# An S4 convolution block with a gated bilinear unit: low powers from exponentials, seeds earlier, the first block's gate on the result, one set of row statistics, and modulation rows behind the first products

## The chip, the cores and the metric

The kernel runs on one core of one Trainium2 chip, in 32-bit floats. The metric is the device time of one execution in microseconds, given as a median over runs. A core has a matrix engine (PE; its weight loads are listed as PEld), a vector engine (DVE), an activation engine (ACT), a general engine (POOL) and a synchronising engine (SP) that here issues nearly all transfers (DMA). Each engine runs its own instructions strictly in order and waits where an operand or a buffer isn't ready yet.

## The reference, cut to what matters

```python
mod = (silu(c) @ w_mod).reshape(1, 6, 1, 640)
sa, ca, ga, sb, cb, gb = (mod[:, i] for i in range(6))
h = layernorm(x) * (1 + ca) + sa                 # x: 2048 x 640
# S4: one kernel of 2048 taps per channel, from 192 complex modes
dt = exp(log_dt); A = A_re + 1j * A_im
K[d, l] = Re(sum_n C[d, n] * exp(dt[d] * A[d, n] * l) * dt[d] * B[d, n])
y = causal_convolution(h, K) + h * Dskip         # over the 2048 rows, by FFT of 4096
x = x + ga * y
h = layernorm(x) * (1 + cb) + sb
x = x + gb * (((h @ w_gate) * (h @ w_up)) @ w_down)   # 640 -> 1536 -> 640
```

## The kernel before, in words

The 640 channels are five blocks (db) of 128. The kernel K is made in 40 steps of 16 channels (n = 0 to 39; a half block hf is four such steps). The power of a mode at tap l is magnitude times phase, and both are split into a low part (l modulo 8) and high parts, so that a step needs only small tables and outer products:

- *Seeds* (`u_seeds`, L597 to L769) prepare a block: rho = dt * A_re and the phase step, the product B*C, its magnitude amp (a root) and its angle (an arctangent), all transposed on PE so that modes lie along partitions. The steps are named by letters and run in the order of the strings SEG0 (block 0, before the main loop) and SEG (later blocks, spread over the loop): `l` loads, `a` rho and phase, `b` and `c` the product B*C and transposes, `u` and `x` the magnitude, `d`/`D` the phase tables DL and DH of half 0 and 1, `r`/`R` the multiples RL and RH of rho, `e`/`E` the exponentials, `f`, `G`, `g`, `h`, `v` amplitude, arctangent and starting phase.
- *Low tables*: LP (seven exponentials of 64*l*rho, on ACT), LH (`tab_ph`, integer phases, POOL) and LQ (`tab_eq`, POOL: amp, amp times the first power, and two doublings). LQ has one copy, so it can only be made after the last use of the one before.
- *Outer products* on POOL (`outer`, L817): Ph (phases, 3.1 us), EQ (3.1 us) and EP (1.65 us) per step n. ACT turns phases into cosine and sine (`trig`, three calls per step: `kg_aq`, `kg_ap`, `kg_b`), DVE multiplies them with EQ and EP (QtA, PtA, PtB, QtB; L872, L878, L898), and PE adds the products up in the bank kg (`kg_ma` L913, `kg_mb` L928). Two PSUM buffers tra and trb take turns for the trig results; Ph, EQ and EP have two copies each.

Meanwhile the layer norm runs over 16 row blocks q: `u_stats` loads block q and takes its statistics on DVE (L568), `row_stats` turns them into reciprocal roots (a root on ACT, between two table loads), `u_hm` normalises on ACT and writes hm to memory. The row blocks from 6 on, loaded once for the statistics and again for the normalising, share three buffers gha, ghb, ghc, in the order a, b, c, a, a, c, a, b, c for blocks 13, 15, 7, 6, 10, 11, 14, (7 again), 12. A load into a buffer waits for the statistics of the block that it replaces.

The modulation vectors come from `mod_l(m)`, which loads 640 columns of w_mod (1.6 MB) into the tables t_tw (m = 2, 0, 4) or t_ti (m = 1, 3, 5), `u_modr`, which multiplies them on PE in two parts (384 and 256 columns, ten products each, L458) and copies the rows out on ACT, and `u_fold`, which turns the rows of m = 0, 1, 2 into columns by 1x1 products (L477), works out shift, gate and their quotients on DVE (L481 to L491) and spreads them again. Rows 3 and 4 follow in `u_modc`.

The transforms (`u_pre` L955, `u_k`, `u_g`, `u_c`, `u_d`) are PE products with activation copies and trips through memory between them; from about 500 us on the gated unit runs on PE almost alone (L1196, L1611).

What runs when is written out by hand in SCHED: each unit is a generator, and each number is the time of one of its steps. The number divided by 1000 is the slot. Slots from -101 on belong to the steps of block 0's seeds, slots 2t and 2t+1 to iteration t of the main loop (three iterations per n), before and after the loop's DVE products:

```python
    for t in range(3 * NK + 24):
        n, g = divmod(t, 3)
        ...
            (kg_aq, kg_ap, kg_b)[g](n)
        due(2 * t)
        ...
            for f in MUL.pop(0):
                f()
        due(2 * t + 1)
        if g < 2 and n + 1 < NK:
            kg_pool(n + 1, g)
```

SLOT lists the buffer that each allocation takes. The order of emission is the order on every queue, SP's included.

## Time and profile before

| | us |
|---|---|
| median of three runs | 992.87 |
| lowest, highest | 990.01, 998.23 |
| the profiled execution's own time | 990.33 |
| its span in the trace | 988.6 |

| engine | busy us | share of the span |
|---|---|---|
| PE | 887.3 | 90% |
| PEld | 726.3 | 73% |
| DVE | 760.7 | 77% |
| ACT | 579.9 | 59% |
| POOL | 577.4 | 58% |

The span leaves out 1.7 us of that execution's time. Times in the lines below are us from the span's start. A line of the timeline has the start, the busy time, the engine, the line of the kernel, the operation, output<-input by the program's names, the tile, and the count where several are merged; in brackets stands how long the engine had been idle and what ended that. A name such as gha is the buffer a of the ring gh. SPq is the issue of a transfer on SP; what a transfer takes is told by those who wait for it.

### The profile page before, as it was taken

Reading aid. Unit: us, or ns where it says so; the run is one execution under the profiler, and the core shown is the slowest. Engines: PE = TensorE matmul, PEld = TensorE weight load, DVE = VectorE, ACT = ScalarE, POOL = GpSimd, SP = SyncE. Lnnn points to the kernel's source line nnn. Section 1 sums busy time; section 2 is a strip of 40 time slices with the busy share of each in tenths; the row PEclk is TensorE's granted clock in tenths of the full one; section 3 lists DMA queues with packets and bytes.
Section 4 is the critical chain, followed back from the end, with each engine's and each line's share of the span. In section 5 each row is a group of like instructions: output and inputs, shape, how many; then the busy total and the mean of one; then the engine's idle time right before and its main releaser. Section 6 shows DMA issues by size and latency. Waiting matters only on the chain.

```text
span 988.6 us, 26668 instructions
## 1 busy us (share of the span) xinstructions
PE 887.3 (90%) x11190; PEld 726.3 (73%) x11190; DVE 760.7 (77%) x1311; ACT 579.9 (59%) x1019; POOL 577.4 (58%) x424
## 2 busy tenths in 40 slices
PE   4854898999798699989988999999999999999998
PEld 3643656676575477677666888889998888889998
DVE  8798479887988977896899877787585977677452
...
GB/s 243 240 172 196 224 211 205 142 138 120 142 151 142 172 155 106 183 187 281 217 102 106 134 186 104 137 159 168 198 134 216 85 80 80 81 54 77 83 161 54
DMA packets 141961, 148.96 MB, mean 151 GB/s; under 512 B 8976, under 2 KB 120080, under 8 KB 140432
## 3 DMA queue, kind: packets, MB, share of 16 engines
...
## 4 chain that ended last, share of the span: by engine, by line
PE 58%; DVE 14%; ACT 13%; issue 6%; POOL 5%; DMA 2%; SPq 0%; DVEq 0%; ACTq 0%; POOLq 0%
PE pa L1196 26%; PE pa L1611 16%; ACT tra L320 2%; ACT trb L320 2%; PE psfb L995 2%; DVE QtA L872 2%; PE psfc L995 2%; PE psfb L1055 1%; PE kg L928 1%; POOL EQ L817 1%; PE psfa L1055 1%; PE kg L913 1%; PE psfc L1055 1%; PE psfb L950 1%; PE psfa L995 1%
## 5 line engine op out<-in xcount | busy, mean ns | idle before, releaser
L817 POOL TENSOR_TENSOR EQ<-LQ,RH 128x1536 f32<-128x1536 f32 x40 | 124.2, 3105 | 15.1 <-DVE QtB L872 14.9
L320 ACT ACTIVATE z<-pa 128x512 f32<-128x512 f32 x24 | 14.4, 599 | 167.1 <-PE pa L1196 120.5
L1160 DVE TENSOR_TENSOR wsgl<-wga,wsgh 128x640 fp32r<-128x640 f32 x72 | 68.1, 948 | 46.8 <-ACT wsgh L320 46.6
L320 ACT ACTIVATE wsgh<-wga 128x640 fp32r<-128x640 f32 x72 | 52.6, 732 | 72.0 <-PE pa L1611 48.6
L1560 POOL TENSOR_TENSOR z<-z,s 128x512 f32<-128x512 f32 x24 | 33.5, 1394 | 98.6 <-DVE s L1559 98.6
L1611 PE MATMUL pa<-wsgh,sh 128*128 128x384 f32 (+1 forms) x304 | 69.6, 310 | 0.0
L1611 PE MATMUL pa<-wsgh,sl 128*128 128x384 f32 (+1 forms) x304 | 69.2, 308 | 0.0
L1611 PE MATMUL pa<-wsgl,sh 128*128 128x384 f32 (+1 forms) x304 | 69.1, 309 | 0.0
L1172 POOL TENSOR_TENSOR tf<-wur,wgb 128x256 f32<-128x256 f32 x24 | 19.2, 801 | 80.7 <-DVE wtl L1160 54.7
L817 POOL TENSOR_TENSOR EP<-LP,RH 128x768 f32<-128x768 f32 x40 | 66.1, 1652 | 0.0
L817 POOL TENSOR_TENSOR Phb<-LH,DH 128x1536 int32<-128x1536 int32 x20 | 62.3, 3113 | 2.2 <-ACT tra L320 2.1
L817 POOL TENSOR_TENSOR Pha<-LH,DH 128x1536 int32<-128x1536 int32 (+1 forms) x21 | 62.4, 2972 | 1.8 <-ACT trb L320 1.4
L872 DVE TENSOR_TENSOR QtA<-tra,EQ 128x1024 f32<-128x1024 f32 x40 | 47.0, 1216 | 17.0 <-ACT tra L320 8.5
L1160 DVE TENSOR_TENSOR wtl<-tf,wth 128x256 fp32r<-128x256 f32 (+1 forms) x72 | 59.9, 858 | 0.0
L872 DVE TENSOR_TENSOR QtA<-trb,EQ 128x1024 f32<-128x1024 f32 x40 | 47.0, 1215 | 12.2 <-ACT trb L320 7.0
L928 PE MATMUL kg<-QtB,PtB 64*32 64x64 f32 x2560 | 47.0, 225 | 8.1 <-DVE QtB L872 8.0
L928 PEld LDWEIGHTS kg<-QtB,PtB 64*32 64x32 f32 x2560 | 40.3, 112 | 15.5 <-DVE QtB L872 9.0
L1558 DVE TENSOR_TENSOR s<-pa,s 128x512 f32<-128x512 f32 x24 | 16.6, 690 | 45.2 <-PE pa L1196 40.1
L1196 PE MATMUL pa<-sl,wth 128*128 128x512 f32 x144 | 45.2, 395 | 2.1 <-DVE sl L1160 2.1
L1611 PEld LDWEIGHTS pa<-wsgh,sl 128*128 128x128 f32 x304 | 46.6, 188 | 0.0
L1611 PEld LDWEIGHTS pa<-wsgh,sh 128*128 128x128 f32 x304 | 46.5, 188 | 0.0
L1611 PEld LDWEIGHTS pa<-wsgl,sh 128*128 128x128 f32 x304 | 46.5, 188 | 0.0
...
## 6 DMA issues: line engine op xcount, KB each, us to landing
...
```

The source lines that it names most:

```text
L320: return S.activation(o, i, f, **kw)
L817: G.tensor_tensor(o.rearrange("p x (h l) -> p x h l", l=8), lo.unsqueeze(2).to_broadcast([P, rows, nh, 8]), hi.rearrange("p h x -> p x h") ...
L872: return [lambda h=h: V.tensor_tensor(Qt[:, :, :, 32 * h : 32 * h + 32], tr[:, ::-1] if h else tr[:, :, :, ::-1], e[:, :, 32 * h : 32 * h ...
L928: PE.matmul(kg[j * 32 : j * 32 + 32, dd, :], PtB[lo : lo + 64, c, r, :], QtB[lo : lo + 64, c, r, :], start=False, stop=dd == 7 and c == 1, ...
L995: PE.matmul(r[c][par * 64 : par * 64 + 64, i, :], t_tw[:, k0 + k, c, :], src[:, k, :], start=True, stop=True, tile_position=(0, par * 64))
L1055: PE.matmul(r[par][:, i], w, v, start=c == 0, stop=c == 1, tile_position=(lo, 0))
L1160: V.tensor_tensor(lo, v, hi, op=OP.subtract)
L1172: G.tensor_tensor(t[:, 0:2], u[:, 0:2], g[:, 0:2], op=OP.subtract)
L1196: PE.matmul(ps, w[a][:, k], x[b][:, l], start=n == 0 and m == 0, stop=n == 2 and m == len(ks) - 1)
L1558: V.tensor_tensor(S67[i], ps, S6[i], op=OP.add)
L1560: G.tensor_tensor(ZT[i], ZT[i], S67[i], op=OP.add)
L1611: PE.matmul(ACC[tb][t][c], x[:, ts], w[:, cs], start=st, stop=f == NF - 1 and n == 2 and (c == 0 or t % 2 == 1))
```

## The change

It has eight parts.

1. LQ is no longer made on POOL. `s_e` gets seven more exponentials (l*rho for l = 1 to 7) in place of one over three multiples of rho, and a new step `q` multiplies them by amp on DVE. `tab_eq` goes; LQ has three copies; RL holds rho alone.
2. The order of block 0's seeds (SEG0): the amplitude and arctangent run earlier, the half 1 tables (`D`) later, and half 1's exponentials (`X`) move from the main loop to the seeds. POOL's outer products EP(1) and EQ(0) and the phases of half 0 are issued inside the seeds, in another order.
3. The statistics of blocks 1, 13, 6, 7, 10 and 15 get later slots, behind the seeds.
4. Modulation products: half of row 1 and all of row 0 move from the seeds to slots 6, 7 and 8 of the main loop, and the loads of w_mod for rows 3 and 4 to slots 6 and 8. The fold moves from slots 11, 12, 19, 22 to 12, 14, 18, 20.
5. One `row_stats` for 16 row blocks in place of two (6 and 10).
6. The gate of block 0 multiplies the result in `u_d` (DVE, in PSUM) and no longer the input in `u_pre` (POOL).
7. `trig` puts the magnitude of the phase into the PSUM buffer that later holds the cosine, where before it had a buffer ab of its own.
8. Smaller: the starting phase of a later block takes three POOL operations for four; temporaries of the seeds share space; three phase tables share a row of zeros.

```diff
@@ -30,24 +30,24 @@
 
 SCHED = dict(
     ml=(-88998, -91999, -98999),
-    mr=(((-87997, 8001), (-87996, 11000)), ((-87999, 2000), (-88997, 8000)), ((-88999, -86998), (-89000, -87998))),
+    mr=(((7000, 11000), (8000, 12000)), ((-87999, 2000), (6000, 9000)), ((-88999, 1100), (-89000, 100))),
     st=(
         (-88993, 5000),
-        (-101000, -92000),
+        (-101000, -87500),
         (5001, 22003),
         (-88996, 15002),
         (-98997, 0),
         (10000, 21002),
-        (-94000, -87995),
-        (-98000, -87994),
+        (-94000, -85900),
+        (-98000, -85800),
         (1000, 20000),
         (1, 19000),
-        (-91998, -87000),
+        (-91998, -85700),
         (-88995, 6000),
         (-87993, 13000),
-        (-99000, -91000),
+        (-99000, -87400),
         (-88994, 16001),
-        (-98998, -86999),
+        (-98998, -85600),
     ),
...
@@ -67,12 +67,11 @@
         (44001, 53002),
         (35002, 43001),
     ),
-    rstd=(22004, 22005),
+    rstd=(22004,),
     tab=(52000, 78002),
-    fo=(11001, 12000, 19001, 22000),
-    e0=(15000,),
+    fo=(12800, 14500, 18001, 20001),
     ds=(32001, 21000, 34000, 43002),
-    mc=((-86997, 21003, 30001, 33001, 37002), (-87992, 39001, 45000, 46001, 48001), (34004, 56000, 60001)),
+    mc=((6500, 21003, 30001, 33001, 37002), (8500, 39001, 45000, 46001, 48001), (34004, 56000, 60001)),
...
-SEG0 = ("l", "a", "b", "c", "ud", "r", "x", "e", "f", "G", "g", "D", "h", "v", "R", "")
-SEG = ("l", "a", "b", "c", "ud", "D", "r", "R", "x", "E", "f", "g", "h", "v")
+SEG0 = ("l", "a", "b", "c", "iud", "r", "x", "e", "f", "Gg", "q", "R", "hv", "DX", "", "Q", "")
+SEG = ("l", "a", "b", "c", "iud", "D", "r", "R", "x", "E", "f", "g", "h", "v")
...
@@ -486,7 +483,6 @@
         V.tensor_tensor(gg, p3[:, 2], g1, op=OP.mult)
-        V.tensor_tensor(sh[:, 0:1], sh[:, 0:1], gg[:, 0:1], op=OP.mult)
         V.tensor_tensor(dt2[:, 1:], dt2[:, 1:], gg[:, 1:], op=OP.mult)
         V.tensor_tensor(dcol[:, 1:], dcol[:, 1:], gg[:, 1:], op=OP.mult)
...
@@ -583,16 +579,17 @@
 
     EQ = [pk1.tile([P, 24, 64], F32, name=f"EQ{i}") for i in range(2)]
     EP = [pk1.tile([P, 24, 32], F32, name=f"EP{i}") for i in range(2)]
-    LQ = pk1.tile([P, 96, 8], F32, name="LQ")
+    LQ = pk1.tile([P, 3, 96, 8], F32, name="LQ")
     LP = pk1.tile([P, 3, 96, 8], F32, name="LP")
     LH = pk1.tile([P, 192, 8], I32, name="LH")
     V.memset(LP[:, :, :, 0], 1.0)
     RH = pk1.tile([P, 3, 11, 96], F32, name="RH")
-    RL = pk1.tile([P, 2, 4, 96], F32, name="RL")
-    DH = [pk1.tile([P, 4, 192], I32, name=f"DH{i}") for i in range(3)]
+    RL = pk1.tile([P, 2, 96], F32, name="RL")
...
@@ -668,29 +664,29 @@
             act(u, x, AF.Square)
             act(q[:, 0], y, AF.Square)
 
+        def s_i():
+            T["st"] = T["q"][:, 1].bitcast(I32).rearrange("p (s r) -> p s r", r=24)
+            V.tensor_copy(T["st"], T["ps"][:, 1])
+
         def s_d(h):
-            ps, q = T["ps"], T["q"]
-            sti = q[:, 1].bitcast(I32).rearrange("p (s r) -> p s r", r=24)
+            ps, sti = T["ps"], T["st"]
             free(h, "lh", "ph")
-            if h == 0:
-                V.tensor_copy(sti, ps[:, 1])
+            if h:
+                V.tensor_tensor(t64, sti, shl[:, 5:6].unsqueeze(2).to_broadcast([P, 8, 24]), op=OP.logical_shift_left)
             V.tensor_copy(g5(Dl[h])[:, 0, :, 1, :], ps[:, 1, hs[h]])
             for a, k0 in ((1, 0), (0, 6)):
                 for D_, n, o in ((Dl[h], 3, 1), (Dh[h], 2, 1)):
                     V.tensor_tensor(g5(D_)[:, o : o + n, :, a, :], sti[:, hs[h]].unsqueeze(1).to_broadcast([P, n, 4, 24]),
                                     shl[:, k0 : k0 + n].unsqueeze(2).unsqueeze(3).to_broadcast([P, n, 4, 24]), op=OP.logical_shift_left)
                     k0 += 3
-            if h:
-                V.tensor_tensor(t64, sti, shl[:, 5:6].unsqueeze(2).to_broadcast([P, 8, 24]), op=OP.logical_shift_left)
             mark("step", 2 * db + h)
 
         def s_r(h):
-            ps = T["ps"]
-            free(h, "ep", "eq", "lq")
-            V.tensor_tensor(g4(Rl[h])[:, 0:3], ps[:, 0, hs[h]].unsqueeze(1).to_broadcast([P, 3, 4, 24]),
-                            mults[:, 11:14].unsqueeze(2).unsqueeze(3).to_broadcast([P, 3, 4, 24]), op=OP.mult)
-            V.tensor_tensor(g4(Rh[h]), ps[:, 0, hs[h]].unsqueeze(1).to_broadcast([P, 11, 4, 24]),
-                            mults[:, 0:11].unsqueeze(2).unsqueeze(3).to_broadcast([P, 11, 4, 24]), op=OP.mult)
+            rho_ = T["ps"][:, 0, hs[h]]
+            free(h, "ep", "eq")
+            V.tensor_copy(Rl[h].rearrange("p (s r) -> p s r", r=24), rho_)
+            V.tensor_tensor(g4(Rh[h]), rho_.unsqueeze(1).to_broadcast([P, 11, 4, 24]),
+                            mults.unsqueeze(2).unsqueeze(3).to_broadcast([P, 11, 4, 24]), op=OP.mult)
 
         def s_u():
             V.tensor_tensor(u, u, T["q"][:, 0], op=OP.add)
...
@@ -702,35 +698,38 @@
             V.tensor_scalar(pe[:, 1], x, 0.0, 0.5, op0=OP.is_ge, op1=OP.subtract)
 
         def s_e(*hh):
-            lp, rh, rl = (halves(R, hh) for R in (LP, RH, RL))
+            lp, lq, rh, rl = (halves(R, hh) for R in (LP, LQ, RH, RL))
             for l in range(1, 8):
-                act(lp[:, :, :, l], rl[:, :, 0], AF.Exp, scale=64.0 * l)
+                act(lp[:, :, :, l], rl, AF.Exp, scale=64.0 * l)
             act(rh, rh, AF.Exp)
-            act(rl[:, :, 0:3], rl[:, :, 0:3], AF.Exp)
+            for l in range(1, 8):
+                act(lq[:, :, :, l], rl, AF.Exp, scale=float(l))
             for h in hh:
                 mark("lp", 2 * db + h)
+
+        def s_q(*hh):
+            lq, a = halves(LQ, hh), T["amp"][:, hh[0] : hh[-1] + 1]
+            V.tensor_copy(lq[:, :, :, 0], a)
+            V.tensor_tensor(lq[:, :, :, 1:8], lq[:, :, :, 1:8], a.unsqueeze(3).to_broadcast([P, len(hh), 96, 7]), op=OP.mult)
+            for h in hh:
+                mark("lq", 2 * db + h)
 
         def s_f():
             pe = T["pe"]
             if db:
                 need(1, "gg")
-            V.scalar_tensor_tensor(amp, u, dt2[:, db : db + 1], pe[:, 1], op0=OP.mult, op1=OP.mult)
             V.scalar_tensor_tensor(pe[:, 0], pe[:, 0], 1e-37, u, op0=OP.max, op1=OP.add)
+            V.scalar_tensor_tensor(u, u, dt2[:, db : db + 1], pe[:, 1], op0=OP.mult, op1=OP.mult)
             V.reciprocal(pe[:, 0], pe[:, 0])
             V.scalar_tensor_tensor(y, y, 2.0, pe[:, 1], op0=OP.mult, op1=OP.mult)
             V.tensor_tensor(pe[:, 0], y, pe[:, 0], op=OP.mult)
             V.tensor_scalar(y, pe[:, 0], 1.0, -1.0, op0=OP.min, op1=OP.max)
 
         def s_G():
-            if db:
-                ps = bank("ps2")
-            else:
-                ps = ring(ps_tr, [P, 2, 512], "tr")[:, :, :N]
+            ps = bank("ps2") if db else ring(ps_tr, [P, 2, 512], "tr")[:, :, :N]
             T["ps2"] = ps.rearrange("p c (s r) -> p c s r", r=24)
-            trans(amp, T["ps2"][:, 0])
-            if db == 0:
-                for h in range(2):
-                    act(g4(Rl[h])[:, 3], T["ps2"][:, 0, hs[h]])
+            T["amp"] = ps[:, 0].rearrange("p (h x) -> p h x", h=2)
+            trans(u, T["ps2"][:, 0])
 
         def s_g():
             if db:
...
@@ -741,26 +740,26 @@
             trans(y, T["ps2"][:, 1])
 
         def s_v():
-            ps = T["ps2"]
             if db:
+                s_q(0, 1)
+            V.tensor_scalar(psi, T["ps2"][:, 1], 4294967296.0 / math.pi, 536870912.0, op0=OP.mult, op1=OP.add)
+
+            def plus(w):
+                G.tensor_tensor(t64[:, w], t64[:, w], psi[:, w], op=OP.add)
+
+            def minus(h):
+                G.tensor_tensor(g5(Dl[h])[:, 0, :, 0, :], t64[:, hs[h]], g5(Dl[h])[:, 0, :, 1, :], op=OP.subtract)
+
+            if db:
+                PSI[2 * db] += [one(plus, slice(0, 8)), one(minus, 0), one(minus, 1)]
+            else:
                 for h in range(2):
-                    V.tensor_copy(g4(Rl[h])[:, 3], ps[:, 0, hs[h]])
-            V.tensor_scalar(psi, ps[:, 1], 4294967296.0 / math.pi, 536870912.0, op0=OP.mult, op1=OP.add)
-
-            def weighted(h):
-                st, s0 = g5(Dl[h])[:, 0, :, 1, :], g5(Dl[h])[:, 0, :, 0, :]
-                G.tensor_tensor(t64[:, hs[h]], t64[:, hs[h]], st, op=OP.subtract)
-                G.tensor_tensor(s0, t64[:, hs[h]], psi[:, hs[h]], op=OP.add)
-
-            for h in range(2):
-                PSI[2 * db + h if db == 0 else 2 * db].append(lambda h=h: weighted(h))
+                    PSI[h] += [one(plus, hs[h]), one(minus, h)]
             mark("seeds", db)
 
         one = lambda f, *a: lambda: f(*a)
-        steps = dict(l=s_l, a=s_a, b=s_b, c=s_c, d=one(s_d, 0), D=one(s_d, 1), r=one(s_r, 0), R=one(s_r, 1), u=s_u, x=s_x,
-                     e=one(s_e, 0), E=one(s_e, 0, 1), f=s_f, G=s_G, g=s_g, h=s_h, v=s_v)
-        if db == 0:
-            LATE.append(lambda: s_e(1))
+        steps = dict(l=s_l, a=s_a, b=s_b, c=s_c, i=s_i, d=one(s_d, 0), D=one(s_d, 1), r=one(s_r, 0), R=one(s_r, 1), u=s_u, x=s_x,
+                     e=one(s_e, 0), X=one(s_e, 1), E=one(s_e, 0, 1), f=s_f, G=s_G, g=s_g, h=s_h, q=one(s_q, 0), Q=one(s_q, 1), v=s_v)
         for i, seg in enumerate(SEG0 if db == 0 else SEG):
             if i:
                 yield
...
@@ -802,16 +801,6 @@
         G.tensor_tensor(lh[..., 1:2], lh[..., 0:1], one(d[1]), op=OP.add)
         double(lh, d[2:], OP.add)
 
-    def tab_eq(hf):
-        need(1, "seeds", hf // 2)
-        if hf:
-            need(1, "eq", 4 * hf - 1)
-        mark("lq", hf)
-        rl = RL[:, hf % 2]
-        G.tensor_copy(LQ[:, :, 0:1], rl[:, 3].unsqueeze(2))
-        G.tensor_tensor(LQ[:, :, 1:2], rl[:, 3].unsqueeze(2), rl[:, 0].unsqueeze(2), op=OP.mult)
-        double(LQ, (rl[:, 1], rl[:, 2]), OP.mult)
-
     def outer(o, lo, hi, rows, nh, op):
 
         G.tensor_tensor(o.rearrange("p x (h l) -> p x h l", l=8),
...
@@ -851,20 +840,21 @@
             mk_ph(n)
             return
         mk_eq(n)
-        mk_ep(n)
+        if n > 1:
+            mk_ep(n)
 
     def trig(src, ab=None):
 
         tr = ring(ps_tr, [P, 2, 512], "tr")
         sv = tr[:, 1, :]
+        cv = tr[:, 0, :]
         if ab is None:
-            ab = pk.tile([P, 512], F32, name="ab", bufs=1)
-            av = ab
+            ab = av = cv
             if len(src.shape) == 3:
                 av, sv = (t.rearrange("p (a x) -> p a x", a=2) for t in (av, sv))
             act(av, src, AF.Abs, scale=TURN)
         act(sv, src, AF.Sin, scale=TURN)
-        act(tr[:, 0, :], ab, AF.Sin, scale=-1.0, bias=halfpi)
+        act(cv, ab, AF.Sin, scale=-1.0, bias=halfpi)
         return tr
 
     def qmul(Qt, tr, e, R):
...
@@ -962,8 +952,6 @@
         SY.dma_start(h, hm[:, 4 * q : 4 * q + 4, db * P : db * P + P])
         yield
         need(1, "sh")
-        if db == 0:
-            G.tensor_tensor(h, h, xa[:, 4, 0:P].unsqueeze(1).to_broadcast([P, 4, P]), op=OP.mult)
         r = [ring(PF[-1], [P, 4, P], "psf") for _ in range(2)]
         d0 = slice(db * P, db * P + P)
         for i in range(2):
...
@@ -1107,6 +1095,8 @@
         mark("d", c)
         if not own:
             need(1, "xr", c, NB - 2)
+        if db == 0:
+            V.tensor_tensor(ps, ps, ggr.unsqueeze(1).to_broadcast([P, 4, P]), op=OP.mult)
         V.tensor_tensor(xs, ps, xs, op=OP.add)
         SY.dma_start(x2d[:, 4 * c : 4 * c + 4, d0], xs)
 
...
@@ -1353,11 +1343,11 @@
         mark("ti")
         SY.dma_start(t_ti.rearrange("p h l m -> p (h l m)"), I["t_ti"])
 
-    def row_stats(q0, q1):
-        need(q1 - q0, "st", q0 == 0)
-        s_ = slice(q0, q1)
-        rstd(mv1[:, s_, :], rs1[:, s_], nm1[:, s_], rv[:, s_], ry[:, s_])
-        mark("rs", q0 == 0)
+    def row_stats():
+        need(10, "st", False)
+        need(6, "st", True)
+        rstd(mv1, rs1, nm1, rv, ry)
+        mark("rs")
 
     def due(x):
         for _, g in sorted(jobs.pop(x, []), key=lambda j: j[0]):
...
@@ -1419,12 +1406,14 @@
             mk_ph(0, 1)
         elif i == P_EP:
             mk_ep(0)
+            mk_ep(1)
+        elif i == P_EQ:
+            mk_eq(0)
+        elif i == P_PSI:
+            tab_ph(0, 0)
+            mk_ph(0, 0)
         elif i == P_MOD:
             mod_i()
-    tab_eq(0)
-    tab_ph(0, 0)
-    mk_ph(0, 0)
-    mk_eq(0)
     for t in range(3 * NK + 24):
         n, g = divmod(t, 3)
         k = n < NK

```

50 lines of the change are left out of this document (23 added, 27 removed).

## The prediction, made before the changed kernel was run

> **What bounds the kernel now.** I read the page's chain first, then the chain for stretches of the span, the busy time by stretch, and the timelines of each queue for the first 100 us, since nearly every edit lies there.
>
> ```profile
> PE 58%; DVE 14%; ACT 13%; issue 6%; POOL 5%; DMA 2%; SPq 0%; DVEq 0%; ACTq 0%; POOLq 0%
> 73.50:150.00 76.50, 57.84 (x1168) 39.77 (x1168) 55.10 (x86) 74.82 (x120) 67.53 (x42) 0.83 0.62 206
> 480.00:988.00 508.00, 493.63 (x2622) 427.46 (x2620) 363.93 (x609) 191.60 (x368) 190.11 (x177) 0.99 0.38 122
> ```
>
> The first line is the chain by engine. The others give, for a stretch, busy us of PE, PE's weight loads, DVE, ACT and POOL, then granted clock, DMA share and GB/s. From 480 on PE is busy 493.6 of 508 us and the change touches nothing there. From 73.5 to 150 ACT is busy 74.8 of 76.5 us: whatever delays ACT's entry into that stretch, or adds to it, delays all that follows. The first 60 us belong to POOL:
>
> ```profile
> by line: POOL EQ L817 16.1%; POOL Phb L817 10.2%; issue 9.8%; POOL Pha L817 7.9%; POOL EP L817 6.9%; POOL LH L777 6.6%; DMA ldt<-A_log_dt 4.2%; DVE st L568 2.8%; DVE DL L680 2.5%; POOL LQ L777 2.4%; DVE psfb L719 2.3%; DVE RH L692 1.9%; POO
> ```
>
> So the change's start (POOL relieved) aims at a real bound there. But other queues run close behind, and the answer lies in them.
>
> **POOL's part.** Rows of POOL, start and duration:
>
> ```profile
> 15.73 1.65 POOL L817 TENSOR_TENSOR EP<-LP,RH 128x768 f32<-128x768 f32 x1
> 17.31 0.36 POOL L811 COPY LQ<-RL 128x96 f32<-128x96 f32 x1
> 18.01 1.51 POOL L777 TENSOR_TENSOR LQ<-LQ,RL 128x192 f32<-128x192 f32 x2
> 26.21 3.09 POOL L817 TENSOR_TENSOR EQ<-LQ,RH 128x1536 f32<-128x1536 f32 x1
> 36.99 3.11 POOL L817 TENSOR_TENSOR Pha<-LH,DH 128x1536 int32<-128x1536 int32 x1
> ```
>
> The low-power table LQ costs POOL 17.31 to 19.52, 2.2 us; ten of them make 22 us. EP(1), 1.6 us, moves into the gap before EQ(0). By queue order EQ(0) then ends near 22.0 instead of 29.3, and phases Pha(0) near 27 (26.3 before), so Ph(1) ends about 2.5 us sooner. That lead is kept only if DVE consumes it.
>
> **DVE's first products come later.** The second half's steps on DVE (L677 to L684, 19.11 to 20.8 below, 1.7 us) now follow q, R and the wait for the transposed arctangent (ACT first does seven more powers, so the arctangent ends near 17.9 instead of 17.4). They end near 21.3, and only then come the row statistics of blocks 1 and 13, which stood ahead of them:
>
> ```profile
> 18.07 0.89 DVE L568 BATCH_NORM_STATS2 st<-gha 128x6 f32<-128x320 f32 x2
> 19.11 0.20 DVE L677 CAST DL<-psfc 128x96 int32<-128x96 f32 x1
> 20.49 0.34 DVE L684 TENSOR_TENSOR ptb<-psfa,shl 128x192 int32<-128x192 int32 x1
> ...
> 18.98 0.33 SPq L560 DMA_DIRECT2D gha<-A_u  x1
> 19.36 0.43 SPq L451 DMA_DIRECT2D t_ti<-w_mod  x1
> ...
> 21.92 0.89 DVE L568 BATCH_NORM_STATS2 st<-gha 128x6 f32<-128x320 f32 x2 [0.82 <-DMA gha<-A_u]
> 22.83 0.33 SPq L560 DMA_DIRECT2D gha<-A_u  x1
> 27.19 0.89 DVE L568 BATCH_NORM_STATS2 st<-gha 128x6 f32<-128x320 f32 x2 [1.50 <-DMA gha<-A_u]
> 30.57 2.31 DVE L872 TENSOR_TENSOR QtA<-trb,EQ 128x1024 f32<-128x1024 f32 x2
> ```
>
> This is a loop through one buffer: statistics free gha, SP loads the next block into it, DVE waits for that. Block 13's statistics end near 23.0 instead of 18.96: 4.0 later. Load 6 goes out then, lands 2.9 later, load 10 after its statistics, landing 4.4 later, and statistics 10, 15 and 4 (3.4 us together) still stand ahead of QtA(0). QtA(0) goes from 30.6 to about 34.6, though its inputs are ready at 26. The t_ti rows queue on SP behind load 6 and come 4.0 later too. The transposed-phase banks and Pha are held until QtA(0) has run, so Pha(2) starts about 1 us late instead of 3.5 early: POOL's lead is gone.
>
> **The fold.** The modulation fold's operations stand on DVE behind PE:
>
> ```profile
> 28.68 3.39 PE L458 MATMUL psfc<-t_ti,sil 128*128 128x384 f32 x10
> 43.39 0.60 PE L477 MATMUL psfb<-ident,TVa 1*128 1x1 f32 x4 [2.45 <-ACT TVa L320]
> 47.22 0.17 DVE L481 TENSOR_SCALAR mcol<-psfb 128x5 f32<-128x5 f32 x1 [2.26 <-PE psfb L477]
> 53.03 1.18 DVE L878 TENSOR_TENSOR PtAa<-tra,EP 128x1024 f32<-128x1024 f32 x1
> ```
>
> Three of six modulation products (3.4 us for 384 columns, by that 2.3 for each of 256) move behind kg(0); with kg's own blocks of 1.1 us PE ends them near 48.7, the last row copy on ACT is near 50.4, the 1x1 products take some 4.2 (in before 43.39 to 47.2, the first few sooner), the DVE operations 2.5 (47.22 to 49.7), so these run 54.6 to 57.2, now ahead of PtA(2). PtA(2) ends near 58 instead of 54.2. Statistics 14, which frees gha for load 8, end 3.75 later.
>
> **SP's queue, the dearest step.** Loads of w_mod for rows 4 and 3 moved from the start to steps 8500 and 6500. They are now behind load 8 and ahead of load 5 (Wb):
>
> ```profile
> 38.64 0.38 SPq L451 DMA_DIRECT2D t_tw<-w_mod  x1
> 51.41 1.40 SPq L451 DMA_DIRECT2D t_ti<-w_mod  x1
> 57.74 0.33 SPq L560 DMA_DIRECT2D gha<-A_u  x1
> 58.59 0.42 SPq L560 DMA_DIRECT2D Wb<-A_u  x1
> 66.33 0.88 DVE L568 BATCH_NORM_STATS2 st<-Wb 128x6 f32<-128x320 f32 x2
> GB/s 259 193 7 0 3 124 331 355 294 321 369 355 376 386 420 399 406 181 65 7 130 389 352 416 365 423 399 420 201 106 273 399 413 413 420 403 413 389 396 399
> ```
>
> The last row is the DMA rate in 40 slices of 5 to 35 us: it tops out near 410. Before, Wb's statistics at 66.33 waited for nothing. Now loads 8 and 2, both tables and load 5 leave together at about 61.9 (57.74 and 3.75, and the issue): blocks of 0.33 MB and tables of 640 x 640 floats, 4.26 MB in all, at 410 is 10.4 us, plus 1.9 for issue and landing (estimate from load 6: 2.9 with 0.8 of transfer): load 5 lands near 74.5 to 75, Wb's statistics are 8.5 later. DVE's seed products, statistics 2 and the root wait behind it in order, and ACT waits for the root:
>
> ```profile
> 70.82 0.21 ACT L320 ACTIVATE ry<-rv 128x6 f32<-128x6 f32 x1
> 72.37 0.21 ACT L320 ACTIVATE ry<-rv 128x10 f32<-128x10 f32 x1 [1.34 <-DVE rv L371]
> 74.83 0.60 ACT L320 ACTIVATE trb<-Pha 128x512 f32<-128x512 int32 x1
> ```
>
> One set of row statistics saves 72.37 less 70.82, 1.5 us, here. ACT enters its saturated stretch 8.5 - 1.5 = 7.0 us late.
>
> **Powers on ACT.** For each later block:
>
> ```profile
> 94.33 2.63 ACT L320 ACTIVATE LP<-RL 128x192 f32<-128x192 f32 x7
> 98.62 0.67 ACT L320 ACTIVATE RL<-RL 128x576 f32<-128x576 f32 x1
> 345.30 2.68 ACT L320 ACTIVATE LP<-RL 128x192 f32<-128x192 f32 x7 [0.20 <-DVE RL L690]
> ```
>
> Seven more of 0.375 (2.63) replace one of 0.67: +2.0 us. At 94 it lies in the saturated stretch, at 345 the chain also runs through LP: +2.0 each. Blocks 2 and 4 have ACT waits beside them: 0 to +2 each, taken as 0. The Trainium skill, "ScalarE: Activation LUTs", What ACT_TABLE_LOAD costs, gives 186 ns + 0.833 ns an element, less 93 of overlap: 0.25 for such a power where the row has 0.375, and by it +1.2 a block; the row decides.
>
> **The rest.**
>
> ```profile
> 24.45 1.25 DVE L692 TENSOR_TENSOR RH<-psfc,mults 128x1056 f32<-128x1056 f32 x1
> 53.90 0.46 ACT L320 ACTIVATE prm<-pta,dt 128x192 f32<-128x192 f32 x1 [3.22 <-DMA pta<-A_A_re]
> 99.99 1.27 POOL L966 TENSOR_TENSOR hfa<-hfa,f16a 128x512 f32<-128x512 f32 x1
> ```
>
> DVE's q step for two halves: a copy and a product of 1344 elements, by RH (1056 elements, 1.25 us) about 1.8, less two copies and two smaller RL (0.8): +1.0 a block, 0 to +4 in all; taken as 0, hidden beside ACT. The gate on the result adds four DVE products of 512 elements (QtA's two of 1024 took 2.31, so 0.6 each) and takes four of 1.27 from POOL's path: -2 to +2.6, taken as 0. The magnitude in PSUM makes ACT wait for its bank half a microsecond sooner: 0 to +3 (five such waits), taken as 0. The exponentials of half 1 leave the main loop, where ACT then stood idle 3.22 us for a load: nothing. LQ gone from POOL in the loop: the chain between 60 and 480 never shows LQ, and its POOL pieces start at a DVE release; 0 to -8, taken as 0.
>
> Sum: 7.0 + 2.0 + 2.0 = +11.0 on the profiled execution's own 990.3 us, 1001.3; call it 1001. The median of the runs, 992.9, is 2.5 above that execution, so this is 0.8% over the median.
>
> **Rivals.** *POOL's lead carries* (faster). If loads 6, 10 and 5 land before DVE asks, so that DVE is not late, POOL sets the pace: -3.5 by Pha(2), -2.2 for LQ(1), -1.5 for the root, +4.0 for ACT: -3.2; with LQ gone ahead of a few later releases, -4 more: 983. For it: the chain of the first 60 us is POOL's. Against: DVE already waits 0.82 and 1.50 for those loads. It decides if QtA(0) starts before 30.6.
>
> *Load 5 overtakes the tables.* If the small load does not queue behind 3.3 MB, 5.3 of the 7.0 go: 996. Against it: load 10, issued 3.5 after t_ti, took 4.4 where load 6 took 2.9.
>
> *The slow clock.* Late, sparse products meet a halved clock:
>
> ```profile
> 40.00:60.00 20.00, 14.10 (x267) 12.97 (x256) 16.83 (x36) 14.85 (x28) 19.53 (x18) 0.66 0.68 235
> 47.11 1.94 PE L913 MATMUL kg<-QtA,PtAb 128*32 128x64 f32 x64
> 39.09 1.10 PE L928 MATMUL kg<-QtB,PtB 64*32 64x64 f32 x64
> ```
>
> kg took 1.94 for 1.10 there. The three late products (8.1) would take 14.2 and the fold, PtA(2) and load 8 come 6 later: 1007, or 1010 with the zeros above at half their upper ends. The Trainium skill, "TensorE: Matmul & The Clock Gate", What's actually happening, says that an idle PE falls to half its clock; the 0.66 agrees.
>
> **How the numbers follow.** Forecast 0.52, slow clock 0.18, overtaking load 0.16, POOL's lead 0.14. A measurement of this kernel tells about 1% from no change, that is 983 to 1003. The forecast spreads 995 to 1007 by its zeros, four tenths of it above 1003; the slow clock is all above; the overtaking load all within; POOL's lead three quarters below. Faster 0.11, within 0.50, slower 0.39. Range 986 to 1010.
>
> **What would show it.** Right: QtA(0) near 34.6 behind a wait for gha; the fold on DVE near 55; Wb's statistics near 75 after several us of waiting on its load; ACT's first sine after the root near 82; fourteen LP and LQ powers of about 0.375 each after it; no LQ on POOL. Wrong: QtA(0) before 31, Wb not waited for, or the ACT stretch starting before 76; and if the shift at 150 us is 9 but the end moves by less than 4, the loop had slack that I denied.

## The result, and the profile after

The changed kernel takes 1029.5 us (median of four runs, 1025.3 to 1031.1), the kernel before on the same chip 995.2: a ratio of 1.034, 95% interval 1.029 to 1.040. The forecast was 1001, with a range of 986 to 1010. The direction was right; the loss is three times what the sum gave.

The profiled execution has a span of 1026.9 us where before had 988.6. First the page's busy times, then the stretch that ACT filled before:

```profile
PE 898.9 (88%) x11190; PEld 735.5 (72%) x11190; DVE 775.3 (76%) x1307; ACT 590.2 (57%) x1051; POOL 552.0 (54%) x376
```

```profile
73.50:150.00 76.50, 48.92 (x866) 34.17 (x870) 48.31 (x85) 63.37 (x102) 49.88 (x27) 0.75 0.62 214
```

POOL lost 25 us of work (577.4 before); DVE and ACT gained 15 and 10, and PE 12 for the same 11190 products (its clock is taken up below). Each is small beside the loss, so most of the new time is waiting. ACT is busy 63.4 us of this stretch, 74.8 before: it enters it late.

To see where the time is lost I take the end of the product PtA of each step n on DVE (start plus duration of its row; before, step 2: 53.03 + 1.18 = 54.2) and subtract that of the kernel before:

| step n | 0 | 2 | 4 | 9 | 15 | 22 | 31 | 39 |
|---|---|---|---|---|---|---|---|---|
| before, us | 34.0 | 54.2 | 81.8 | 135.9 | 196.0 | 279.5 | 371.0 | 445.0 |
| after, later by | 5.2 | 10.9 | 15.5 | 19.5 | 26.8 | 30.2 | 35.8 | 39.1 |

From step 39 to the end both take the same (988.6 - 445.0 = 543.6 and 1026.9 - 484.0 = 542.9). So all of it is lost in the seeds and the main loop: before step 0, at step 2, at step 4, around each later block's seeds (steps 6, 14, 22, 30), and little by little between these places.

The timeline of DVE after, first the statistics loop through gha, then the fold and the wait for load 5:

```profile
22.44 0.89 DVE L564 BATCH_NORM_STATS2 st<-gha 128x6 f32<-128x320 f32 x2
26.33 0.89 DVE L564 BATCH_NORM_STATS2 st<-gha 128x6 f32<-128x320 f32 x2 [1.88 <-DMA gha<-A_u]
32.38 0.89 DVE L564 BATCH_NORM_STATS2 st<-gha 128x6 f32<-128x320 f32 x2 [3.75 <-DMA gha<-A_u]
35.75 2.31 DVE L862 TENSOR_TENSOR QtA<-trb,EQ 128x1024 f32<-128x1024 f32 x2
...
54.30 0.11 DVE L478 TENSOR_SCALAR mcol<-psfb 128x5 f32<-128x5 f32 x1
54.45 0.17 DVE L479 TENSOR_SCALAR mcol<-mcol 128x5 f32<-128x5 f32 x1
54.65 1.57 DVE L480 TENSOR_TENSOR mcol<-mcol 128x5 f32<-128x5 f32 x1
56.26 3.02 DVE L481 TENSOR_SCALAR mcol<-mcol 128x5 f32<-128x5 f32 x1
59.31 1.56 DVE L482 TENSOR_TENSOR mcol<-mcol 128x5 f32<-128x5 f32 x1
60.91 0.19 DVE L483 RECIPROCAL mcol<-mcol 128x5 f32<-128x5 f32 x1
61.13 0.16 DVE L484 TENSOR_TENSOR mcol<-psfb,mcol 128x5 f32<-128x5 f32 x1
61.21 0.15 DVE L485 TENSOR_TENSOR mcol<-psfb,mcol 128x5 f32<-128x5 f32 x1
61.40 2.53 DVE L486 TENSOR_TENSOR dt<-dt,mcol 128x4 f32<-128x4 f32 x1
63.93 1.21 DVE L868 TENSOR_TENSOR PtAa<-tra,EP 128x1024 f32<-128x1024 f32 x1
...
83.34 0.89 DVE L564 BATCH_NORM_STATS2 st<-Wb 128x6 f32<-128x320 f32 x2 [7.17 <-DMA Wb<-A_u]
```

The loop and QtA of step 0 came as forecast (35.75; forecast 34.6). The fold began where forecast (54.3; 54.6), but took 9.6 us, not 2.5: operations on four or five elements a partition took 1.6 to 3.0 us. Load 5 was waited for as forecast, but at 83.3, not 75, since all was late already. Behind it ACT waited for the root's input; its first sine of the stretch comes at 90.3, before at 74.83, where I had 82:

```profile
85.94 0.36 ACT L316 ACTIVATE ptb<-ptb 128x192 f32<-128x192 f32 x1 [10.70 <-issue]
...
87.84 0.21 ACT L316 ACTIVATE ry<-rv 128x16 f32<-128x16 f32 x1
...
90.30 0.60 ACT L316 ACTIVATE trb<-Pha 128x512 f32<-128x512 int32 x1
```

POOL's rows beside the fold:

```profile
53.62 2.59 POOL L776 TENSOR_TENSOR LH<-LH,DL 128x384 int32<-128x384 int32 x2
56.16 3.09 POOL L806 TENSOR_TENSOR EQ<-LQ,RH 128x1536 f32<-128x1536 f32 x1
59.21 1.64 POOL L806 TENSOR_TENSOR EP<-LP,RH 128x768 f32<-128x768 f32 x1
60.81 3.10 POOL L806 TENSOR_TENSOR Pha<-LH,DH 128x1536 int32<-128x1536 int32 x1
```

Each long operation of the fold ends within 0.03 us of the POOL operation beside it: L480 at 56.22 (LH 56.21), L481 at 59.28 (EQ 59.25), L482 at 60.87 (EP 60.85), L486 at 63.93 (Pha 63.91). The two that read psfb, in PSUM, took 0.16 and 0.15 beside Pha; so did the reciprocal (0.19), with its one operand in SBUF.

ACT and then DVE at the second block's seeds, after and before:

```profile
196.25 2.67 ACT L316 ACTIVATE LP<-RL 128x192 f32<-128x192 f32 x7
198.71 1.96 ACT L316 ACTIVATE RH<-RH 128x2112 f32<-128x2112 f32 x1
200.58 2.68 ACT L316 ACTIVATE LQ<-RL 128x192 f32<-128x192 f32 x7
...
209.62 0.50 DVE L712 COPY LQ<-psfc 128x192 f32<-128x192 f32 x1
209.96 1.55 DVE L713 TENSOR_TENSOR LQ<-LQ,psfc 128x1344 f32<-128x1344 f32 x1
211.69 1.21 DVE L868 TENSOR_TENSOR PtAa<-tra,EP 128x1024 f32<-128x1024 f32 x1
```

```profile
178.95 0.68 ACT L320 ACTIVATE RL<-RL 128x576 f32<-128x576 f32 x1
...
186.41 0.41 DVE L747 COPY RL<-psfc 128x96 f32<-128x96 f32 x2
187.00 1.21 DVE L878 TENSOR_TENSOR PtAa<-tra,EP 128x1024 f32<-128x1024 f32 x1
```

Seven powers (2.68) stand where one exponential (0.68) stood, and behind them on DVE, ahead of PtA, stand a copy and a product where two copies stood: 1.8 us and 0.33, each counted to the start of the operation behind them (211.42 and 186.74).

### The profile page after: what moved, and what is told of

It reads as the page before. It is cut to its first block, busy times and chain, and to the rows that moved or that the text cites. A ratio compares the mean times of both kernels' runs of the same rounds, so it can differ in the third digit from the quotient of the medians.

```text
span 1026.9 us, 26647 instructions
## 1 busy us (share of the span) xinstructions
PE 898.9 (88%) x11190; PEld 735.5 (72%) x11190; DVE 775.3 (76%) x1307; ACT 590.2 (57%) x1051; POOL 552.0 (54%) x376
## 5 line engine op out<-in xcount | busy, mean ns | idle before, releaser
L862 DVE TENSOR_TENSOR QtA<-trb,EQ 128x1024 f32<-128x1024 f32 x40 | 47.0, 1218 | 16.8 <-ACT trb L316 7.6
L918 PEld LDWEIGHTS kg<-QtB,PtB 64*32 64x32 f32 x2560 | 40.5, 112 | 15.6 <-DVE QtB L862 8.4
```

The source lines that it names most:

```text
L862: return [lambda h=h: V.tensor_tensor(Qt[:, :, :, 32 * h : 32 * h + 32], tr[:, ::-1] if h else tr[:, :, :, ::-1], e[:, :, 32 * h : 32 * h ...
L918: PE.matmul(kg[j * 32 : j * 32 + 32, dd, :], PtB[lo : lo + 64, c, r, :], QtB[lo : lo + 64, c, r, :], start=False, stop=dd == 7 and c == 1, ...
```

## The experiments

Theories: (A) the fold's DVE operations are held by the POOL operations beside them; (B) load 5 behind the tables sets the start of ACT's stretch (my dearest step); (C) the powers cost on ACT and on DVE one behind the other, in every block; (D) DVE's first products are late for the loop through gha; (E) the magnitude in PSUM costs where ACT waits for the bank. Rival to all: the loop has slack, and a local delay is absorbed or only moved. Ratios are to the kernel before on the same chip, with 95% intervals.

**e1_load5: load 5 ahead of the tables.** `st[5]: (10000, 21002) -> (5002, 21002)`

> The changed kernel with one load moved: block 5 (buffer Wb) is loaded in slot 5, ahead of the two w_mod tables of rows 3 and 4, instead of in slot 10 behind them. Theory (transfers of one queue are served in order, so that load 5 waited for 3.3 MB of tables): DVE's wait of 7.2 us ahead of Wb's statistics goes, PtA(4) ends 5.5 to 7 us sooner than the changed kernel's 97.3, and that carries to the end: about 1023. Rival (DVE waited for something else, or the transfers share the engines and the small one would not have been late): the wait stays above 4 us and the end moves by less than 2.

1029.7 us, 1.035 [1.028, 1.043]: no gain, against my theory. DVE in this run:

```profile
76.22 0.87 DVE L564 BATCH_NORM_STATS2 st<-Wb 128x6 f32<-128x320 f32 x2
...
89.95 2.36 DVE L862 TENSOR_TENSOR QtA<-trb,EQ 128x1024 f32<-128x1024 f32 x2 [5.96 <-PE kg L903]
```

and PE:

```profile
81.11 6.47 PE L455 MATMUL psfc<-t_ti,sil 128*128 128x384 f32 x10 [9.22 <-DMA t_ti<-w_mod]
...
88.69 1.10 PE L903 MATMUL kg<-QtA,PtAb 128*32 128x64 f32 x64
```

Wb is no longer waited for, and QtA waits 5.96 us instead, for PE, where the product of row 3 stands ahead of kg and waits for its table. The same late tables are met by another engine: (B) is right about the queue, not about what its removal is worth.

**e2_foldpsum: the fold's intermediates in PSUM.** Two results go to the fold's own bank, and two copies bring them to SBUF:

```diff
-        g1, sg, rg, sh, gg = (mcol[:, i, :] for i in range(5))
+        g0, sg, rg, sh, gg = (mcol[:, i, :] for i in range(5))
+        g1, gp = (pc[:, 64 + 8 * i : 64 + 8 * i + NB] for i in range(2))
...
-        V.tensor_tensor(gg, p3[:, 2], g1, op=OP.mult)
-        V.tensor_tensor(dt2[:, 1:], dt2[:, 1:], gg[:, 1:], op=OP.mult)
-        V.tensor_tensor(dcol[:, 1:], dcol[:, 1:], gg[:, 1:], op=OP.mult)
+        V.tensor_copy(g0, g1)
+        V.tensor_tensor(gp, p3[:, 2], g0, op=OP.mult)
+        V.tensor_copy(gg, gp)
+        V.tensor_tensor(dt2[:, 1:], dt2[:, 1:], gp[:, 1:], op=OP.mult)
+        V.tensor_tensor(dcol[:, 1:], dcol[:, 1:], gp[:, 1:], op=OP.mult)
```

> The changed kernel with the modulation fold's intermediates in PSUM, so that none of its DVE operations has two operands in SBUF; two small copies are added. Theory (in the changed kernel these operations of 128x5 elements took 1.5 to 3.0 us each because each waited until the POOL instruction running beside it had ended): they take 0.1 to 0.4 us each again, the fold takes about 2.5 us for 9.6, PtA(2) ends near 58 for 65.1, and the end is 5 to 7 us sooner, about 1023. Rival (they are slow for another reason, the small size or the waits between them): they stay above 1 us wherever POOL runs.

1017.1 us, 1.023 [1.015, 1.030]: 12 us less than after. DVE in this run (the first, a middle and the last operation of twelve):

```profile
53.98 0.15 DVE L479 TENSOR_SCALAR psfb<-psfb 128x5 f32<-128x5 f32 x1
...
54.57 0.17 DVE L482 TENSOR_SCALAR psfb<-psfb 128x5 f32<-128x5 f32 x1
...
55.83 0.15 DVE L490 TENSOR_TENSOR dcol<-dcol,psfb 128x4 f32<-128x4 f32 x1
55.89 1.22 DVE L871 TENSOR_TENSOR PtAa<-tra,EP 128x1024 f32<-128x1024 f32 x1
...
75.13 0.89 DVE L567 BATCH_NORM_STATS2 st<-Wb 128x6 f32<-128x320 f32 x2 [6.98 <-DMA Wb<-A_u]
```

Twelve operations take 1.9 us where ten took 9.6; PtA of step 2 is 8.0 earlier, and step 11 still 8.2. (A) holds. Step 39 is 11.4 earlier; the other 3.1 come between steps 11 and 15, far behind the fold. There PE's granted clock differs between the two traces, first after, then e2:

```profile
170.00:178.00 8.00, 7.31 (x123) 6.39 (x124) 7.49 (x19) 6.68 (x12) 7.92 (x4) 0.57 0.79 236
```

```profile
162.00:170.00 8.00, 6.73 (x204) 5.82 (x203) 7.97 (x20) 7.49 (x14) 7.92 (x5) 1.00 0.81 245
```

At 0.57 a kg of 64 products took 1.93 us there, at 1.00 1.10, and DVE waited for kg twice (0.47 and 0.53) where in e2 it didn't. With the fold as short as I had put it, Wb's statistics come at 75.1, the time that I forecast.

**e3_both: e1 and e2 together.**

> The changed kernel with both edits: load 5 ahead of the tables, and the fold's intermediates in PSUM. Theory: the two losses lie one behind the other on the same chain and add up, 11 to 13 us of the 36 go, about 1017; PtA(4) ends near 85 for 97.3. Rival (one hides the other): no more than the larger of the two alone, about 1023.

1022.2 us, 1.027 [1.022, 1.032]: not better than e2 alone. The two don't add up. QtA waits 5.74 us for kg, again behind the product of row 3; and in this trace the first of the late products, half of row 1, ran at a granted clock of 0.50 and took 4.55 us for the 2.43 of e2, so that step 2 is 3.8 us later than there.

**e4_before_fold14: the kernel before with its fold's DVE part in slot 14.** `fo: (11001, 12000, ...) -> (11001, 14500, ...)`

> The kernel before with one number changed: the DVE step of the modulation fold in slot 14 instead of slot 12, so that it meets POOL's outer products of 1.6 to 3.1 us instead of its small table operations. Theory (these DVE operations wait for the POOL instruction beside them): the fold's DVE operations stretch from 2.5 us to 6 to 10, PtA(2) ends 4 to 8 us later than 54.2 and the end is 3 to 7 us later, about 997. Rival (it is the changed kernel's other parts that make them slow): they keep 2.5 us and nothing moves by more than 2.

998.3 us, 1.004 [1.001, 1.007]; span 996.8. The fold runs from 52.9 to 63.0, and step 2 is 9.9 us late, step 39 8.5:

```profile
53.07 3.10 DVE L482 TENSOR_SCALAR mcol<-mcol 128x5 f32<-128x5 f32 x1
...
59.92 3.07 DVE L491 TENSOR_TENSOR dcol<-dcol,mcol 128x4 f32<-128x4 f32 x1
```

So the slot alone makes the delay at step 2, with nothing else of the change. At the end it is worth 4 us by the ratio and 8.5 in the trace. The kernel before had been lucky in its slot: it ran the fold beside POOL's short operations.

**e5_front: e2, and load 8 behind the tables (slot 8600 for 1000),** so that the tables leave at 57, where they left at 61.5 in e2 and at 69.5 in after.

> The changed kernel with the fold's intermediates in PSUM, and with load 8 moved behind the two w_mod tables, so that SP can issue the tables some 14 us sooner than where they stood behind load 8. Moving load 5 alone had taken DVE's wait away, but PE then waited as long for the product of row 3, which needs one of the tables. Theory (the tables' late issue is the cost, by whichever of the two waits): both waits go, PtA(4) ends near 83 for 97.3 and 89.1 with the fold alone, and the end is 5 to 7 us sooner than with the fold alone: about 1011. Rival (a third wait takes their place): PtA(4) stays within 2 of 89 and the end near 1017.

1017.4 us, 1.024 [1.016, 1.031]: as e2, and a miss. Wb isn't waited for and step 4 is 1.9 us earlier than in e2, but step 2 is 3.6 later, and step 39 1.4 later. The delay at step 2 isn't the edit's (e3, without it, has it too): the first late product ran slow on PE, and the fold waited 1.32 us for its inputs. The product in e2, then in e5:

```profile
39.96 2.43 PE L455 MATMUL psfb<-t_ti,sil 128*128 128x256 f32 x10
```

```profile
40.47 4.53 PE L455 MATMUL psfb<-t_ti,sil 128*128 128x256 f32 x10
```

The granted clock from 40 to 45 us is 1.00 in e2 and 0.52 in e5. In e6 and e7, which have the same front, it is 1.00 (2.42 us for the product) and step 4 is 2.8 and 3.8 us late, for 7.3 in e2. So the late tables, my dearest step, cost some 4 us at step 4. At the end e5 shows nothing of it; its trace also loses 3.1 us to e2 between steps 11 and 15, at a clock of 0.57 (160 to 168 us) for 1.00.

**e6_lqpool: e5 with LQ of the later blocks on POOL again.** `tab_eq` and its slots come back for half blocks 2 to 9, one exponential for the seven, two copies for the product.

> The kernel with both front repairs (fold in PSUM, tables ahead of load 8), in which blocks 2 to 5 of the channels get their low-power table LQ on POOL again, as in the kernel before: the seven extra exponentials on ACT and the product on DVE go, one exponential over three multiples and POOL's doublings come back. Theory (ACT and DVE stand one behind the other on the chain at each block's seeds, 2.0 and 1.75 us a block, and POOL's 2.2 a half block are hidden): 10 to 14 us sooner than the kernel with both front repairs, about 998 to 1001; the jumps of PtA around steps 5, 13 to 15, 21 and 29 to 31 go. Rival (POOL's relief pays for part of it): less than 6.

1004.0 us, 1.009 [1.007, 1.012]: 13.4 less than e5. Step 15 was 16.8 late and is 7.1, step 39 29.1 and is 13.5. But e5's trace is a poor measure: 2.6 of the 15.6 stand at step 4 already, and between steps 11 and 15 e6 runs at a clock of 1.00, as e2 does. Against e2, step 4 is 4.5 earlier and step 39 14.2, so that some 10 are left for the powers behind step 4. (C) holds in the main: +2.0 on ACT and +1.5 on DVE are 3.5 a block, 14 in four, of which 13 show by the ratio and 10 in this trace. The edit takes both off together, so how much is ACT's and how much DVE's isn't shown.

**e7_ownab: e5 with the magnitude of the third trig call in PtB's buffer.**

> The kernel with both front repairs, in which the third trig call of a step puts the phase's magnitude into the buffer of PtB instead of the PSUM bank that the sine goes to. Theory (in the bank, the magnitude must wait until DVE has read the bank's last contents, so 0.5 us of ACT can't be done ahead; over 40 steps some of it lies on the chain): 2 to 4 us sooner than the kernel with both front repairs, most of it between steps 31 and 39 where the changed kernel lost 3 more. Rival (ACT is late anyway): within 1.

1015.5 us, 1.021 [1.014, 1.027]: 2 less, inside the interval. In the trace step 39 is 3.9 earlier, but step 2 is 2.9 earlier already, for the clock: this prices nothing.

**e8_lqab: e6 and e7 together.**

> The changed kernel with four of its steps altered at once: the fold's intermediates in PSUM, load 8 behind the two tables, LQ of the later blocks on POOL again, and the magnitude of the third trig call in a buffer of its own. If the powers on the chain (13.4 us by the run with LQ on POOL) and the magnitude in PSUM (2 to 4 us) are separate terms, this is 1000 to 1002 us, 0.6 to 0.9% over the kernel before, and the shift stays flat from step 31 to step 39. If the magnitude's cost comes only because the loop is late from the powers, it stays at 1004.

1009.3 us, 1.014 [1.009, 1.019], no better than e6: missed. PtB isn't a buffer of its own, as `ab` was: PE reads it for kg, and ACT now waits for that (3.25 us at step 21 in e10). So this edit can't price (E).

**e9_gatein: e5 with the gate on the input, on POOL, again.**

> The kernel with both front repairs, in which block 0 is gated at the input on POOL again (four products of 512 elements, 1.27 us) and no longer at the result on DVE (four of about 0.65). Theory (DVE is nearer to the chain than POOL there): 0 to 2 us sooner than the kernel with both front repairs. Rival (POOL's four products delay the transforms of block 0): 1 to 4 us later.

1018.1 us, 1.023 [1.017, 1.030]: the gate makes no difference that shows.

**e10_oldstats: e8 with the six statistics in their slots of before.** `st: (-101000, -87500) -> (-101000, -92000)` and five like it.

> The kernel with those four steps altered, and besides the statistics of blocks 1, 6, 7, 10, 13 and 15 in their slots of before. Theory (the loop load, statistics, load through the buffer gha makes DVE's first product late): QtA of step 0 starts near 31 instead of 35, steps 0 and 1 are 4 us earlier, and the end comes 3 to 5 us earlier, near 997. Rival (POOL, not DVE, sets the pace once step 2 is reached, or the statistics now delay the seeds on DVE instead): step 0 moves by less than 2 us, or the lead is gone by step 4, and the end is that of the run without this edit, near 1001.

1001.3 us, 1.008 [1.005, 1.010]; QtA of step 0 starts at 31.9 (35.75 after), and step 39 is 4.9 earlier than in e8. (D) holds, for 6 us by the ratios of e8 and e10, 2 to 3 by those of e6 and e15 below, the latter inside the interval.

**e11_before_foldpsum: the kernel before with the fold in PSUM. e12_before_fold_rs: the same with one set of row statistics.**

> The kernel before with only the fold's intermediates in PSUM. In that kernel the fold runs from 47.2 to 49.7 us in about 2.5 us beside POOL, with few operations held. Theory: two copies more, some operations shorter; PtA of step 2 within 1 us of the kernel before, the end within 2 us of it, either way: the fold costs much only where POOL's outer products run beside it.

> The kernel before with the fold's intermediates in PSUM and one set of row statistics in place of two (the one part of the change that I counted as a gain: 1.5 us between the two roots on ACT). Theory: the first sine after the root comes 1.5 us earlier and the shift stays, so the end is 1 to 2 us under the run with the fold in PSUM alone. Rival: the root's step waits for something else (the statistics of the last block), so nothing moves and the end is within 0.5 us of that run.

993.7 us, 0.998 [0.996, 1.001], and 991.3, 0.997 [0.995, 0.999]. The one set of statistics brings step 4 forward by 1.8 us (forecast 1.5). e12 is the only version that beats both kernels beyond its interval, by 0.3%.

**e13_oldmod: e10 with part 4 undone. e14_before_latemod: e12 with part 4, load 8 behind the tables.**

> The run with the old statistics' slots, and besides the modulation products, the loads of rows 3 and 4, load 8 and the fold in their slots of before (the fold's intermediates stay in PSUM). What is left of the change is the new order of block 0's seeds with LQ by exponentials there, the gate on the result, one set of row statistics, the smaller parts. If part 4 makes the remaining loss: 991 to 994 us, no slower than before. If the new seeds or the gate make it: 999 to 1002, as without this edit.

> The kernel before with the fold's intermediates in PSUM, one set of row statistics, and part 4 of the change: half of row 1 and all of row 0 multiplied in slots 6 to 8, the loads of rows 4 and 3 in slots 6 and 8 (load 8 behind them), the fold in slots 12, 14, 18 and 20. If part 4 makes the remaining loss: 998 to 1002 us, PtA of step 4 some 3 us later than before and the shift grows behind it while PE works at a lower clock. If not: 991 to 993, as without part 4.

1000.8 us, 1.004 [1.003, 1.006], and 992.3, 0.998 [0.995, 1.000]. With the fold out of POOL's way and the tables ahead of load 8, moving the modulation products costs nothing that shows, in either kernel; what remains in e10 lies in the rest.

**e15_oldstats_psum: e10 with the magnitude in PSUM. e16_before_magpsum: e12 with the magnitude in PSUM.** The edit of e16:

```diff
+        cv = tr[:, 0, :]
         if ab is None:
-            ab = pk.tile([P, 512], F32, name="ab", bufs=1)
-            av = ab
+            ab = av = cv
...
-        act(tr[:, 0, :], ab, AF.Sin, scale=-1.0, bias=halfpi)
+        act(cv, ab, AF.Sin, scale=-1.0, bias=halfpi)
```

> The run with the old statistics' slots, but with the magnitude of the third trig call in PSUM as the change has it, in place of PtB's buffer. If PtB's buffer cost some 3 us there: about 998 us, 0.4 to 0.5% over before. If the magnitude in PSUM costs as much as PtB's buffer: 1001, as with it.

> The kernel before with the fold's intermediates in PSUM, one set of row statistics, and the magnitude of the third trig call in PSUM. ACT writes the magnitude only when the bank is free, half a microsecond of work that it did before while it waited for the bank. If this costs (five waits of half a microsecond and more by the trace of before): 993 to 996, 2 to 4 over the run without it (991.3). If ACT has slack at those places: 991 to 992.

1001.7 us, 1.006 [1.003, 1.009], and 999.0, 1.004 [1.002, 1.006], where e12 had 0.997: (E) is worth 7 us in the kernel before. In the changed kernel e15 is as e10, so the bank costs no more there than PtB's buffer, and the price isn't known apart. ACT in e12 and in e16, waits from 75 to 485 us (us in total, times, longest), then one such place, in e12 and in e16:

```profile
ACT trb L320 <- DVE QtA L875: 3.0, 1, 3.0
...
ACT tra L320 <- DVE QtA L875: 2.5, 2, 1.6
```

```profile
ACT trb L320 <- DVE QtA L875: 4.6, 5, 3.0
ACT tra L320 <- DVE QtA L875: 4.6, 6, 2.1
```

```profile
261.93 0.60 ACT L320 ACTIVATE tra<-Phb 128x512 f32<-128x512 int32 x1 [1.63 <-DVE QtA L875]
```

```profile
265.34 1.24 ACT L320 ACTIVATE tra<-Phb 128x512 f32<-128x512 int32 x2 [2.13 <-DVE QtA L875]
```

In e12 ACT waits for a bank that QtA holds at three places (5.5 us), in e16 at eleven (9.2), and in the merged row the magnitude and the sine (1.24) both stand behind the wait; in e12 the magnitude had been taken before it. Eleven times 0.6 us is 6.6; that this makes the 7 is a sum that fits and no more, since the trace of e16 is of its slowest execution (1002.4 us). The changed kernel itself has eleven such waits (9.7 us), the kernel before four (5.4), e15 twelve.

Step by step, us later than the kernel before:

| step n | 0 | 2 | 4 | 9 | 15 | 22 | 31 | 39 |
|---|---|---|---|---|---|---|---|---|
| e2 | 4.9 | 2.9 | 7.3 | 11.3 | 15.5 | 18.9 | 24.4 | 27.7 |
| e5 | 4.6 | 6.5 | 5.4 | 9.5 | 16.8 | 20.2 | 25.8 | 29.1 |
| e6 | 4.8 | 3.8 | 2.8 | 6.4 | 7.1 | 7.1 | 11.5 | 13.5 |
| e10 | 1.4 | 1.9 | 2.1 | 3.6 | 4.8 | 8.0 | 8.9 | 9.9 |
| e12 | 0.0 | 1.4 | -0.9 | 2.1 | 2.8 | 1.7 | 1.3 | 1.1 |

From step 4 on the shift grows in every row but e12's, and hardly any of it is given back: the loop has little slack (I had said none). It has some: e12 gives 1.7 us back behind step 15. By ratios, the 3.4% divide into 1.2 for the fold (after to e2), 1.4 for the powers (e5 to e6), 0.3 for the statistics (e6 to e15), and 0.6 that is left in e15, no more than the 0.7 of the magnitude alone (e12 to e16). The single ratios are good to 0.2 to 0.8 either way, so a part, a difference of two of them, is good to some 3 to 9 us; the first two and the magnitude are clear of that, the statistics' 0.3 isn't, and the table bears the first two out at their places. By these ratios nothing that shows is left for the gate, the late tables and the new order of the seeds together; by the traces some 4 us of the tables may be among the parts.

## Why the prediction was wrong

- **"The fold" (its 2.5 us): wrong, 12 us by the ratios, 8.2 of them the fold's own in the trace.** I took the duration of the DVE operations from their rows in before and moved it to another time. The rows in before held the warning, which I had not quoted:

```profile
47.42 0.43 DVE L482 TENSOR_SCALAR mcol<-mcol 128x5 f32<-128x5 f32 x1
47.88 0.30 DVE L483 TENSOR_TENSOR mcol<-mcol 128x5 f32<-128x5 f32 x1
48.22 0.17 DVE L484 TENSOR_SCALAR mcol<-mcol 128x5 f32<-128x5 f32 x1
...
49.19 0.48 DVE L489 TENSOR_TENSOR mcol<-mcol 128x1 f32<-128x1 f32 x1
```

The same shape takes 0.17 and 0.43, and one element a partition 0.48; POOL, in the gap after Phb, then ran operations of 0.4 to 0.7 us. At 54 to 64 POOL runs operations of 1.6 to 3.1. A duration that varies so within one shape has a wait in it, and here it grew with what ran beside it. The Trainium skill, "SBUF — State Buffer", SBUF: two separate sides, states that the port pair which DVE and GpSimd (POOL here) share is an exclusive lock held for a whole instruction, and that a DVE operation needs it in a two-port mode or, against a GpSimd operation that reads SBUF, with two SBUF inputs. I left this rule out. After agrees with it in the operations with two SBUF inputs (1.57, 1.56 and 2.53 us), e2 in those with one in PSUM (0.15 to 0.17). The TENSOR_SCALAR that took 3.02 us in after and 3.10 in e4 has one input; that it ran in a two-port mode no trace shows, nor that the hold is at a port.

- **"The rest", DVE's q step "hidden beside ACT", and "Powers on ACT", 0 for two of the four blocks: wrong, 10 to 13 us for four.** The two follow each other: the arctangent waits for ACT's powers, the q step for its turn on DVE, and PtA stands behind the q step. I had the sizes (2.0 and 1.0 a block; the rows have 2.0 and 1.5) and found cover in an average: ACT's waits somewhere in the stretch. At the place itself there was none.

- **"The rest", the magnitude in PSUM "taken as 0": wrong, 7 us (in the kernel before, e12 to e16).** I counted five waits in before. But this edit lets ACT do less ahead of a wait, and the wait then binds at more places: eleven in e16 and eleven in after. Its upper end of 3 was too low.

- **"SP's queue, the dearest step": the mechanism right, its worth wrong.** The tables left ahead of load 5 and Wb's statistics waited 7.17 us. Undone, in e1 and e5, it gave nothing that shows at the end: in e1 PE met the same tables at row 3's product (9.22), in e5 a slow clock hid the gain of some 4 us at step 4 that e6 and e7 show. I had put 7.0 of my 11.0 there. The rival that load 5 overtakes the tables is out: in after load 5 is issued at 70.54 and landed at 83.3. A small slip beside it: by load 6 (2.9 less 0.8) the issue and landing take 2.1 us, not 1.9.

- **"DVE's first products come later": right** (35.75 for 34.6, the loads waited for 1.88 and 3.75). It is worth 2 to 6 us at the end (the 2 isn't clear of the interval); I had no term of its own for it, since I let it end in the wait for load 5.

- **"POOL's part": right.** POOL ended EQ of step 0 early (it starts at 18.9) and lost the lead to DVE, so the rival in which the lead carries is out. The gate at nothing held (e9), and the one set of row statistics gave 1.8 for 1.5 (e11 to e12).

- **The slow clock: not where I had put it, but not out either.** In after the three late products ran at a granted clock of 1.00 (2.43, 3.39 and 2.43 us from 40.3 to 49.3), so the rival's 14.2 us for them didn't come. Elsewhere the clock did cost: row 3's product took 5.26 us, after 6.68 of waiting for its table and at a grant of 0.66 (75 to 85 us), for 3.49 in before; the stretch from 170 to 178 us makes the 3.1 us between e2 and after, as far as the traces tell; and half of row 1 ran slow in the traces of e3, e5, e8 and e9 (4.1 to 4.6 us for 2.4) and not in those of e1, e2, e6, e7 and after. The mean grant from 73.5 to 150 us alone says little: 0.75 in after and 0.83 in before, but 0.80 in e15 and 0.79 in e12, which takes no longer than before. How much of the whole loss is the clock's no run shows.

Of my 11.0, 7.0 stood for the queue, which is worth some 4 at step 4 and nothing that shows in the end times of e1 and e5, and 4.0 for the powers, which measured 10 to 13; the fold's hold, the magnitude and the first products had no term and measured 8 to 12, 7 and 2 to 6. These parts make 27 to 38 where 34 were lost, but they come from different pairs of runs, so that the sum closes is no proof. That I had the direction is in part luck: the step that carried most of my sum carries little or nothing of the loss. What is left open: how much of each part is the clock's, and what the magnitude costs in the changed kernel by itself.
